# Queries computed ahead of keys and values, with their exponentials kept in memory

## The chip, the cores and the metric

The kernel runs on one core of a Trainium2 chip. A core has five engines with instruction queues of their own: TensorE (matrix products, PE in the profile, with PEld for its weight loads), VectorE (DVE), ScalarE (ACT), GpSimd (POOL) and SyncE (SP), which here only starts DMAs. The metric is the device time of one execution in microseconds; the time given is the median of several.

## The reference

For 2048 tokens of width 1024, normed to `xn`, the kernel computes a linear attention with 32 heads of width 32 and a gated feed-forward block of width 3584, and joins them:

```
q, k, v = xn @ wqkv                        # 32 heads of width 32
pq, pk  = q @ w_phi, k @ w_phi             # a 32x32 matrix for each head
phi(p)  = [softmax(p), softmax(-p)]        # 64 features for each head
kv, z   = phi(pk)^T v, sum over tokens of phi(pk)
o       = phi(pq) kv / (phi(pq) . z + 1e-6)
s       = o @ wo
g       = silu((silu(xn @ w1) * (xn @ w3)) @ w2)
out     = x + s * g
```

Everything is float32. Products run in three passes over a high and a low part of each operand (`PASSES`, `split` on lines 88 to 93): high times high, high times low, low times high, so one 128x128 block times 512 columns is three matmuls.

## The kernel before

The work goes through stages, all written out by a Python program, so every instruction has a line but no loop is left on the chip.

**Seven products.** Large products use a scheme with seven block products instead of eight (`ORDER`, line 61). The left operand of a pair of token tiles and the right operand of a pair of column halves are turned into seven sums each, named A11 ... S4 and B11 ... T4; the seven products accumulate in three PSUM banks a, b, c, and between them ScalarE copies and VectorE additions read the banks.

**Gate and up** (`gate_up`, from line 588). For each half of the tokens (`tb`) and each of 28 column blocks (`f`), seven products of twelve matmuls. Beside them runs side work, hung on event numbers by a planner: `room` (line 436) puts work only where VectorE's planned load of one product stays below 2.55 us, `at` (line 387) hangs a function on an event. The side work norms and turns the second half of x, folds `w_phi` into the key and query weights (`side_fold`), and prepares the seven sums of the key and value weights (`side_kv`), of `w2` (`side_w2`) and the high and low parts of `wo` (`side_split`), all stored in memory. Normed x is also stored plainly (`store_x`, `xn_d`).

**Keys and values** (`heads`, line 800). Two passes (`c` = 0, 1) over eight pairs of tiles. Each pair has seven products of twelve matmuls; then key features (`keys`: maximum, minimum, exponentials, sums) and the small products `kv` (line 790) with 32-column groups of TensorE. `reload` fetches x for the next pair, `fetch` the seven weight operands, 2 MB each, of the next pass.

**Down projection** (`product`, line 1031). Seven blocks `kb` over eight pairs, six matmuls a product. In the last block, tiles are gated as they come ready (`gate`: silu, stored to `g_d`) and weights of the last stage are loaded into ring slots (`ring`, line 873). Two query projections for the first tile stand among these products.

**Last stage** (lines 1179 to 1203). For each of 16 tiles: project the queries (`project_q`, 24 matmuls for each half of the columns, in the plain way with eight block products), make their features and denominators (`queries`), turn these with TensorE's transposes (`turn_e`), multiply them by the small key-value matrices (`attend`, 64x32 pieces) and finish: project with `wo` (24 matmuls a half), multiply by the gate, add x, store (`finish`).

**Order.** Where nothing is said, a scheduler orders each engine's instructions by program order and its own cost estimates. `in_order(...)` (line 47) makes the named engines follow the program text. Line 1141 does so for SyncE and TensorE; line 1202, after the first tile, leaves TensorE alone in that mode:

```
        if i == 1:
            in_order(ENG.PE)
```

An instruction waits in its engine's queue until its operands are ready, and what stands behind it waits too. That holds for SyncE's DMA starts.

Of the kernel before, what the change touches and what calls it, by code (L numbers as in the profile page):

```python
# [17 lines left out]
P = 128  # L18
# [3 lines left out]
G = 8  # L22
# [7 lines left out]
def tile_kernel(ctx: ExitStack, tc: tile.TileContext, x, wkT, wqT, wv, wphi, wo, w1, w3, w2, out):  # L30
# [39 lines left out]
    xn_d = dram.tile([P, ND, S], F, name="xn_d")  # L70
# [5 lines left out]
    wkv_d = [{n: dram.tile([P, 2, 4, 512], F, name=f"wkv_d{c}{n}") for n in BNAMES} for c in range(2)]  # L76
# [4 lines left out]
    wqo_d = [[dram.tile([P, 2, 512], F, name=f"wqo_d{c}_{k}") for k in range(ND)] for c in range(2)]  # L81
# [3 lines left out]
    z_d = dram.tile([1, 2, 4, 4, 2, DH], F, name="z_d")  # L85

# [8 lines left out]
    def project(ps, xT, w, tag="mm"):  # L95

        p = ps.tile([P, 512], F, name="pm", tag=tag, bufs=3 if tag == "mm" else BANKS["a"])
# [52 lines left out]
    HOMES = [(4, 5, 6, 0, 1, 3, 2), (7, 8, 4, 5, 6, 0, 1), (2, 3, 7, 8, 4, 5, 6), (0, 1, 2, 3, 4, 5, 6)]  # L150
# [74 lines left out]

    def store_x(t, hf, xf):
        nc.sync.dma_start(xn_d[:, 4 * hf:4 * hf + 4, t * P:(t + 1) * P], xf)
# [113 lines left out]
    def first_turn(t, h):  # L341
        q, n = t % 4, ("A11", "A12", "A21", "A22")[t // 4 * 2 + h]
        raw[q][n] = raw_x(turn(xs[t][h]), room_a[:, q] if n == "A21" else None)
        store_x(t, h, raw[q][n])
# [111 lines left out]
    def side_x(i, s0):  # L456
# [18 lines left out]
        for m, (n, j, hf) in enumerate((("A11", 0, 0), ("A12", 0, 1), ("A21", 1, 0), ("A22", 1, 1))):  # L475
            at(s1 + m, lambda n=n, j=j, hf=hf: pts.update({n: turn(xt[j][hf])}), before)
            at(s1 + m, lambda n=n: a.update({n: raw_x(pts[n])}))
            at(s1 + m + 2, lambda n=n, j=j, hf=hf: store_x(pairs[i][j], hf, a[n]))
# [10 lines left out]
    def side_kv(c, k, s0):  # L489
# [8 lines left out]
        for n in BNAMES:  # L498
# [3 lines left out]
            at_ = store_quad(at_ + 1, wkv_d[c][n][:, :, k], lambda src=src: (r + t2)[src], "wkvo", then)  # L502

    def side_fold(m, s0):
# [4 lines left out]
        if m < 16:  # L509
            at(s0 + 5, lambda: nc.scalar.copy(flat(w[0]), w[1]))  # L510
            at(s0 + 7, lambda: nc.sync.dma_start(d, flat(w[0])))
        else:
            store_quad(s0 + 5, wqo_d[c][k], lambda: w[1], "wqo")

    def side_split(d, src, s0):
        r = []

        def load():
            r.append(blk2())
# [5 lines left out]
    def side_w2(kb, kk, s0):  # L525
        r = []

        def load():
            r.extend(blk2() for _ in range(4))
            for h in range(2):  # L530
                f = 4 * kb + 2 * kk + h
                for n in range(2):
                    nc.sync.dma_start(r[h + 2 * n], w2[f * P:(f + 1) * P, n * 512:(n + 1) * 512])
# [4 lines left out]

        at(s0, load)
        at_ = room(s0 + 4, 2 * OP_US)  # L540
        at(at_, sums)
        for n in BNAMES:
# [3 lines left out]
            at_ = store_quad(at_ + 1, w2_d[kb][n][:, kk], lambda src=src: r[src], "w2o", then)  # L546
# [12 lines left out]
    for m in range(8):  # L559
        side_kv(m // 4, m % 4, FIRST_STEP + 59 + 11 * m)  # L560
    for m in range(28):
        side_store(m, FIRST_STEP + 45 + 4 * m)

    for u in range(2 * NKB):
# [678 lines left out]
```

## Time and profile before

| what | value |
|---|---|
| median of 3 runs | 2425.21 us (2424.5 to 2426.57) |
| span of the profiled execution | 2423.0 us, mean granted TensorE clock 0.999 |
| TensorE busy | 2394.2 us (99%) |
| VectorE busy | 1770.7 us (73%) |
| ScalarE busy | 881.3 us (36%) |
| GpSimd busy | 192.5 us (8%) |
| DMA | 517.87 MB, mean 214 GB/s |

The profiled execution's own time is its span, first to last instruction; the median stands 2.2 us above it. In a row of a timeline the columns are the start in us, the length in us, engine, line, operation, out<-in and the count of merged instructions; in brackets stand the idle time before and what ended it. In a row of the groups by line the columns are line, engine, operation, shapes and count, then busy us and the mean ns of one, then idle time before and what ended it. In a row by stretch of time: the stretch, its length, busy us (and count) of PE, PEld, DVE, ACT, POOL, then granted clock, share of the DMA engines and GB/s. A row of DMA issues has out<-in, queue, count, KB each and us to landing. Matmuls are pipelined: the distance between two starts, not the length of one, is what one costs.

### The profile page before, as it was taken

What the parts mean: (1) busy time and instruction counts of PE and PEld (TensorE: products, weight loads), DVE (VectorE), ACT (ScalarE), POOL (GpSimd) and SP (SyncE); (2) the same over time, 40 slices, a digit from 0 to 9 for tenths busy, and PEclk for the clock granted to TensorE, in tenths of its full rate; (3) what the DMA queues carried; (4) which work ended last, traced back from release to release, by engine and by line L of the source; (5) the groups of instructions that cost most, each with busy time, mean ns of one, the idle gap of its engine ahead of it and who ended that gap; (6) DMA issues with size and microseconds to landing.
All of it is one profiled execution on the core that took longest, in us unless ns stands there. A gap on an engine that the chain in (4) does not pass through costs nothing. (4 is left out here: it accounts for less than half of the span.)

```text
span 2423.0 us, 35675 instructions
## 1 busy us (share of the span) xinstructions
PE 2394.2 (99%) x13650; PEld 1970.2 (81%) x13650; DVE 1770.7 (73%) x2887; ACT 881.3 (36%) x1550; POOL 192.5 (8%) x158
## 2 busy tenths in 40 slices
PE   7999999999999999999999999999999999999998
PEld 6788888888888888888787888888888887888886
DVE  8877787875688878764555666678888777777775
ACT  6445444443454444442111114322222243222221
POOL 1000000000000000000000000011111112222332
PEclk9999999999999999999999999999999999999999
DMA  7456899996788876656858745442445476222221
GB/s 281 158 184 224 267 345 336 323 320 218 242 308 297 309 271 238 240 220 246 332 177 345 248 155 202 174 169 89 152 174 182 153 260 226 79 86 89 75 84 70
DMA packets 293227, 517.87 MB, mean 214 GB/s; under 512 B 18752, under 2 KB 167104, under 8 KB 291264
## 3 DMA queue, kind: packets, MB, share of 16 engines
q1 hardware_dynamic: 293056, 515.59, 61.2%
q8 instruction: 108, 1.77, 0.3%
q14 instruction: 63, 0.52, 0.1%
HBM read 329.65 MB, written 185.87 MB: 213 GB/s over the span
## 5 line engine op out<-in xcount | busy, mean ns | idle before, releaser
L93 DVE TENSOR_TENSOR bo<-rw,bo 128x512 fp32r<-128x512 f32 x336 | 230.7, 689 | 158.3 <-ACT bo L92 157.5
L92 ACT CAST bo<-rw 128x512 fp32r<-128x512 f32 x336 | 206.3, 617 | 6.2 <-DMA xo_d1S<-xoS 3.6
L1042 PE MATMUL bankb<-bo,as 128*128 128x512 f32 x816 | 200.9, 389 | 0.0
L101 PE MATMUL pm<-wq,xh 128*128 128x512 f32 x768 | 181.1, 392 | 0.0
L1042 PEld LDWEIGHTS bankb<-bo,as 128*128 128x128 f32 x816 | 153.2, 188 | 31.8
L101 PEld LDWEIGHTS pm<-wq,xh 128*128 128x128 f32 x768 | 143.1, 188 | 32.0 <-issue 2.8
L615 PE MATMUL bankb<-op0S,bo 128*128 128x512 f32 x672 | 163.0, 391 | 1.9 <-ACT op0S L92 1.1
L615 PE MATMUL bankc<-op0S,bo 128*128 128x512 f32 x672 | 162.6, 391 | 0.3 <-DVE op0S L93 0.3
L615 PE MATMUL bankb<-op1S,bo 128*128 128x512 f32 x672 | 161.2, 389 | 0.0
L615 PE MATMUL bankc<-op1S,bo 128*128 128x512 f32 x672 | 161.2, 389 | 0.0
L615 PE MATMUL bankb<-op0A,bo 128*128 128x512 f32 x672 | 159.7, 392 | 0.9 <-DVE bo L93 0.5
L615 PE MATMUL bankb<-op1A,bo 128*128 128x512 f32 x672 | 157.5, 389 | 0.1
L615 PEld LDWEIGHTS bankb<-op0S,bo 128*128 128x128 f32 x672 | 125.2, 188 | 28.5 <-ACT op0S L92 1.6
L615 PEld LDWEIGHTS bankb<-op1A,bo 128*128 128x128 f32 x672 | 126.0, 188 | 27.0 <-DVE u L657 0.9
L615 PEld LDWEIGHTS bankb<-op1S,bo 128*128 128x128 f32 x672 | 126.1, 188 | 26.2
L615 PEld LDWEIGHTS bankc<-op1S,bo 128*128 128x128 f32 x672 | 126.1, 188 | 26.2
L615 PEld LDWEIGHTS bankb<-op0A,bo 128*128 128x128 f32 x672 | 125.1, 188 | 27.0 <-DVE bo L93 0.8
L615 PEld LDWEIGHTS bankc<-op0S,bo 128*128 128x128 f32 x672 | 125.3, 188 | 26.4 <-DVE op0S L93 0.7
L101 PE MATMUL pm<-wos,oT 128*128 128x512 f32 x576 | 142.2, 397 | 4.2 <-DVE oT L93 2.7
L1042 PE MATMUL bankc<-bo,as 128*128 128x512 f32 x576 | 146.2, 389 | 0.0
L101 PEld LDWEIGHTS pm<-wos,oT 128*128 128x128 f32 x576 | 107.9, 190 | 33.3 <-DVE oT L93 9.3
L1042 PEld LDWEIGHTS bankc<-bo,as 128*128 128x128 f32 x576 | 108.1, 188 | 22.4
(233 smaller groups left out, 4245.2 us busy)
## 6 DMA issues: line engine op xcount, KB each, us to landing
rw<-in_w SPq DMA_DIRECT2D x112, 512.0 KB, 4.5
hr<-h_d SPq DMA_DIRECT2D x56, 512.0 KB, 3.6
h_d<-h SPq DMA_DIRECT2D x111, 256.0 KB, 4.6
xoS<-xo_d0S SPq DMA_DIRECT2D x32, 512.0 KB, 8.2
xoS<-xo_d1S SPq DMA_DIRECT2D x32, 512.0 KB, 3.6
room<-in_w SPq DMA_DIRECT2D x56, 256.0 KB, 6.0
xoA<-xo_d0A SPq DMA_DIRECT2D x24, 512.0 KB, 7.7
xoA<-xo_d1A SPq DMA_DIRECT2D x24, 512.0 KB, 3.5
```

What stands on the lines that cost most here:

```text
L92: nc.scalar.copy(hi, src)
L93: (by or nc.vector).tensor_sub(lo, src, hi.bitcast(F))
L101: nc.tensor.matmul(p, xT[dch][:, a], w(dch, b), start=n == 0, stop=n == 3 * ND - 1)
L615: nc.tensor.matmul(bank[b], bos[tb, f][bn][:, w, k], ao[an][:, u, k], start=first and n == 0, stop=LAST[b] == an and n == 11, skip_group_c ...
L1042: nc.tensor.matmul(bank[b], t[:, u, pos + k], bos[kb, bn, k][:, w], start=first and n == 0, stop=LAST[b] == an and n == 5, skip_group_chec ...
```

## The change

Queries get a stage of their own, ahead of keys and values, by seven products. `side_fold` stores the folded query weights plainly; four units of `side_w` (which takes the place of `side_w2`) turn them into seven sums in the second half of gate and up, among the fourteen units for `w2`. The splits of `wo` move to the first half. Normed x is no longer stored plainly. The stage loop runs over `c` = 0 (queries), 1, 2 (keys and values), with `HOMES` and `NEXT` saying which slot and which moment each operand gets.

For each pair of tiles `query_heads` makes four feature blocks; `query_features` takes maximum and minimum, subtracts (on GpSimd for three blocks of four), takes exponentials, sums them, keeps the ratio `rho` of the two sums, and stores exponentials (`e_d`, 1 MB a tile) and `rho`.

The last stage projects no queries. `load_e` loads a tile's exponentials, `prep` multiplies them by z on GpSimd, sums on VectorE, scales, and turns them in 32x32 blocks with VectorE's transpose. The first two tiles are prepared in the last block of the down projection. `attend` works on a batch of two or four tiles and one half of the columns, with 32x32 pieces, in four PSUM banks (`bufs=1`). SyncE and TensorE follow the program text through the whole stage.

```diff
+    def query_features(i, j, c, p, rho, eng):
+        e = e_rooms[j][:, c].rearrange("p (h s f) -> p h s f", s=2, f=DH)
...
+        nc.vector.tensor_reduce(mm[:, 0, :], p3, axis=AX.X, op=OP.max)
+        nc.vector.tensor_reduce(mm[:, 1, :], p3, axis=AX.X, op=OP.min)
+        eng.tensor_sub(e[:, :, 0], p3, mm[:, 0, :].unsqueeze(2).to_broadcast([P, 16, DH]))
+        eng.tensor_sub(e[:, :, 1], mm[:, 1, :].unsqueeze(2).to_broadcast([P, 16, DH]), p3)
+        nc.scalar.activation(ef, ef, AF.Exp)
+        nc.vector.tensor_reduce(sums.rearrange("p h s -> p (h s)"), ef.rearrange("p (n f) -> p n f", f=DH),
+                                axis=AX.X, op=OP.add)
+        nc.vector.reciprocal(rho[:, j, c], sums[:, :, 1])
+        nc.vector.tensor_mul(rho[:, j, c], sums[:, :, 0], rho[:, j, c])
+        nc.sync.dma_start(e_d[pairs[i][j]][:, c], ef)
...
-    late_splits = [(wqo_d[c][k], d) for _, k, c, d in folds[16:FOLDS]]
...
+    for k in range(4):
+        units.insert(4 * k + 3, ([wq_d[n][k + 4 * h] for n in range(2) for h in range(2)],
+                                 lambda n, k=k: wkv_d[0][n][:, :, k]))
+    for u, (srcs, dst) in enumerate(units):
+        side_w(srcs, dst, HALF + 4 + 8 * u)
...
-    for c in range(2):
+    NEXT = ({0: 2, 1: 3, 2: 4, 3: 5, 4: 6}, {0: 2, 1: 3, 2: 4, 3: 5, 6: 6}, {})
+    for c in range(3):
...
-            pend = heads(i, xo, wb, steps(), pend)
+            if c:
+                pend = heads(i, xo, wb, steps(), pend)
+            else:
+                query_heads(i, xo, wb, steps())
...
+    def load_e(t):
+        rhos[t] = own[0][:, 512 + 32 * (t % 4):544 + 32 * (t % 4)].rearrange("p (c h) -> p c h", c=2)
+        i, j = next((i, p.index(t)) for i, p in enumerate(pairs) if t in p)
+        nc.sync.dma_start(rhos[t], rho_d[i][:, j])
+        for c in range(2):
+            nc.sync.dma_start(e_slab(t, c), e_d[t][:, c])
+
+    def prep(t):
...
+        for c in range(2):
+            nc.gpsimd.tensor_mul(ez[c], e_slab(t, c), zb[c])
+        for c in range(2):
+            nc.vector.tensor_reduce(z[:, c].rearrange("p h s -> p (h s)"), ez[c].rearrange("p (n f) -> p n f", f=DH),
+                                    axis=AX.X, op=OP.add)
+        nc.vector.tensor_mul(den, z[:, :, :, 1], rho)
+        nc.vector.tensor_add(den, den, z[:, :, :, 0])
+        nc.vector.reciprocal(by[:, :, :, 0], den)
+        nc.vector.tensor_mul(by[:, :, :, 1], by[:, :, :, 0], rho)
+        for c in range(2):
+            e3 = e_slab(t, c).rearrange("p (n f) -> p n f", f=DH)
+            nc.vector.tensor_mul(e3, e3, by[:, c].rearrange("p h s -> p (h s)").unsqueeze(2).to_broadcast([P, H, DH]))
+            nc.vector.transpose(et_slab(t, c), e_slab(t, c))
...
+    def attend(tiles, c):
+        n = len(tiles)
+        po = ps.tile([P, 4, 512], F, name="po", bufs=1)
...
+        for k in range(4):
+            for s in range(2):
+                for j in range(4):
+                    for a in range(4):
+                        sl = slice(32 * a, 32 * a + 32)
+                        nc.tensor.matmul(ev[32 * j:32 * j + 32, a, k], kvr[c][sl, j, s, k], et[sl, :, 4 * k + j, s],
+                                         start=s == 0, stop=s == 1, skip_group_check=True)
...
+    def finish(i, c):
+        cs = slice(c * 512, c * 512 + 512)
+        g, xr = (work.tile([P, 512], F, name=name, tag="w") for name in ("g", "xr"))
+        nc.sync.dma_start(g, g_d[i][:, cs])
+        nc.sync.dma_start(xr, x[i * P:(i + 1) * P, cs])
+        p = project(ps, [oTs[i, h][:, :, k] for h in range(2) for k in range(4)], lambda k, a: wos[c, k][:, a])
+        nc.vector.tensor_mul(g, p, g)
+        (nc.vector if i + 1 == NT else nc.gpsimd).tensor_add(g, g, xr)
+        nc.sync.dma_start(out[i * P:(i + 1) * P, cs], g)
...
-        if i == 1:
-            in_order(ENG.PE)
...
+    def prepare(upto):
+        nonlocal ahead
+        while ahead < upto:
+            prep(ahead)
+            if ahead + 2 < NT:
+                load_e(ahead + 2)
+            ahead += 1
+
+    batches = [[0, 1], [2, 3], [4, 5], [6, 7], [8, 9, 10, 11], [12, 13, 14, 15]]
+    for c in range(2):
+        attend(batches[0], c)
+    done = 2
+    for tiles, later in zip(batches, batches[1:] + [None]):
+        for t in tiles:
+            for c in range(2):
+                if later and t == tiles[-1]:
+                    prepare(later[-1] + 1)
+                    attend(later, c)
+                    if c:
+                        done = later[-1] + 1
+                elif c == 0:
+                    prepare(min(ahead + 1, done + 6, NT))
+                finish(t, c)
```

More of the change, by code (lines that the diff above doesn't have):

```diff
@@ L1137, in tile_kernel @@
     ps = pool("ps4", 3, space=PSUM)
-    gate(*pairs[-1])
-    for k in range(14, 16):
-        load_wo(k, accp.tile([P, 2, 512], R, name="wos", tag="accW", bufs=2))
+    gate(len(pairs) - 1)
     in_order(ENG.SP, ENG.PE)
-    def turn_e(e, q):
-        pt = ps.tile([P, 4, P], F, name="pt2", tag="tr", bufs=3)
-        for g in range(4):
-            nc.tensor.transpose(pt[:, g, :], e[:, (4 * q + g) * P:(4 * q + g + 1) * P], ident)
-        et = work.tile([P, 4, P], F, name="et", tag="w")
-        nc.scalar.copy(et, pt)
-        return et
```

306 lines of the change are left out of this document (139 added, 167 removed).

## The prediction

> **What bounds the kernel now.** The page first: TensorE against the span.
>
> ```profile
> span 2423.0 us, 35675 instructions
> PE 2394.2 (99%) x13650; PEld 1970.2 (81%) x13650; DVE 1770.7 (73%) x2887; ACT 881.3 (36%) x1550; POOL 192.5 (8%) x158
> ```
>
> TensorE is the bound: taking matmuls away pays, as long as what replaces them keeps pace. So I read TensorE's timeline for stage borders and pitch, and the chain of waits for the end.
>
> ```profile
> 1133.71 2.88 PE L810 MATMUL bankb<-op2B,xoA 128*128 128x512 f32 x12
> 1303.69 3.01 PE L810 MATMUL bankb<-op3B,xoA 128*128 128x512 f32 x12
> 1391.46 2.88 PE L810 MATMUL banka<-op3B,xoA 128*128 128x512 f32 x12
> 1394.18 2.88 PE L810 MATMUL bankb<-op3T,xoS 128*128 128x512 f32 x12
> 1472.17 1.65 PE L1042 MATMUL bankb<-bo,af 128*128 128x512 f32 x6
> 1991.53 5.60 PE L101 MATMUL pm<-wq,xh 128*128 128x512 f32 x24
> 1996.97 1.52 PE L1042 MATMUL bankc<-bo,as 128*128 128x512 f32 x6
> 2018.12 5.60 PE L101 MATMUL pm<-wq,xh 128*128 128x512 f32 x24
> ```
>
> ```profile
> 2406.90 11.47 PE pm L101 x48
> 2418.45 0.70 DVE gx L1175
> ```
>
> Twelve matmuls take 2.72 us (1394.18 - 1391.46), a projection of 24 takes 5.44 (1996.97 - 1991.53). Gate and up end at 1133.7, keys and values at 1472.2, and the last stage runs from 2018.1 to 2418.4: 400.3 us, the stage this change rewrites.
>
> Next SyncE, with VectorE and GpSimd beside it, for the first tile of that stage, where SyncE's order is written by hand.
>
> ```profile
> 2046.32 0.34 SPq L1177 DMA_DIRECT2D out<-gx  x1
> 2046.70 0.43 SPq L1172 DMA_DIRECT2D gx<-g_d  x1
> 2047.18 0.46 SPq L1173 DMA_DIRECT2D gx<-in_x  x1
> 2052.34 0.34 SPq L1177 DMA_DIRECT2D out<-gx  x1
> ```
>
> ```profile
> 2050.22 0.69 DVE L1175 TENSOR_TENSOR gx<-pm,gx 128x512 f32<-128x512 f32 x1 [2.13 <-DMA gx<-g_d]
> ```
>
> ```profile
> 2051.04 1.27 POOL L1176 TENSOR_TENSOR gx<-gx 128x512 f32<-128x512 f32 x1 [4.75 <-DVE gx L1175]
> ```
>
> The loads of one half tile go out only after the store of the half before (2046.32, 2046.70): load, multiply, add, store, 6.0 us from store to store. TensorE needs 5.44 for the half, and VectorE sat 2.13 us for the load. Before the change this loop closes once, since SyncE's written order ends after the first tile. The diff drops that release (`if i == 1: in_order(ENG.PE)`), so the loop closes 32 times.
>
> **The change, part by part.** Terms are in the time of the profiled execution, 2423.0; the median, 2425.2, lies 2.2 higher, which I add at the end.
>
> *Gate and up.* The stores of normed x and the split query folds go; 16 splits of `wo` move to the first half, and four more units of seven quads and four sums enter the second.
>
> ```profile
> 340.00:360.00 20.00, 20.00 (x98) 16.86 (x97) 16.96 (x27) 10.32 (x19) 0.00 (x0) 1.00 1.07 383
> 860.00:980.00 120.00, 120.00 (x530) 99.06 (x529) 97.61 (x153) 57.11 (x107) 0.00 (x0) 1.00 0.77 264
> 1303.00:1313.00 10.00, 10.00 (x106) 8.37 (x106) 8.40 (x12) 2.39 (x4) 0.13 (x1) 1.00 1.01 429
> 1863.00:1939.00 76.00, 76.00 (x337) 62.95 (x336) 61.11 (x105) 20.38 (x41) 10.19 (x9) 1.00 0.42 150
> ```
>
> ```profile
> L93 DVE TENSOR_TENSOR w2o<-room,w2o 128x512 fp32r<-128x512 f32 x98 | 67.0, 684 | 0.0
> L1011 POOL TENSOR_TENSOR ez<-e,zb 128x1024 f32<-128x1024 f32 x32 | 77.3, 2416 | 211.9 <-issue 137.9 <-ACT e L1010 74.0
> L1019 DVE TENSOR_REDUCE sums<-ez 128x32 f32<-128x1024 f32 x32 | 39.0, 1220 | 39.5 <-POOL ez L1011 39.5
> L1025 DVE TENSOR_TENSOR e<-e,by 128x1024 f32<-128x1024 f32 x32 | 39.1, 1222 | 0.6
> L1023 DVE RECIPROCAL by<-rho 128x16 f32<-128x16 f32 x32 | 8.1, 253 | 1.1
> L1021 DVE TENSOR_TENSOR rho<-sums,rho 128x16 f32<-128x16 f32 x32 | 5.6, 174 | 1.0
> L795 PE MATMUL pkv<-ev 128*32 128x34 f32 x2048 | 24.6, 199 | 1.8 <-DVE ev L835 1.8
> L1159 PE MATMUL po<-et,kvu 64*32 64x128 f32 x1024 | 21.0, 277 | 0.3 <-ACT et L1150 0.3
> ```
>
> The units add 44 VectorE instructions of 0.68 us, 30, against 11 of the splits that leave. VectorE idles 22 us in each 120 there (97.6 busy), over some 460 us: cover enough, 0 us. If it were gone, 19 us would show. In the first half 16 subtractions come and 16 go, and DMA is already full in places (share 1.07); a late weight block could cost up to 5. Bounds 0 to 5; I take 0, since TensorE is busy throughout even in that row.
>
> *Queries by seven products.* A new stage of 8 pairs x 7 products x 2.72 = 152.3. Its cover: VectorE per pair has three adds, eight 512-wide reductions and two subtractions at 0.68, four 1024-wide reductions at 1.22 and eight small ones near 0.2, 15.5 us of TensorE's 19.0; if that slips, up to 8 x 2 = 16. Of GpSimd's six subtractions a pair (1.27, as at 2051.04) nothing waits but an exponential. The stored exponentials lie in the rooms of the key features; their last stores end some 5 us into the key stage, whose first use of them by TensorE comes after seven products: 0. Keys and values keep their work but no longer enter from gate and up: the first half took 170.0 against the second's 168.5, so -1.5; the entry stall is passed to queries, +1.
>
> At the hand-over to keys the operands of the next stage come in: seven of 2.1 MB, with 3.7 MB of x, while the exponentials (16 stores of 1 MB in all, 2.1 MB a pair) leave. In the row at 1303 the same hand-over already fills DMA (share 1.01, 429 GB/s) and just fits. The two last pairs now add 4.2 MB: 4.2 / 0.42 = 10 us; the earlier fetches of the diff give back some. I take 9; bounds 0 to 13.
>
> *Down projection.* Two query projections leave: -10.9. Two tiles are prepared there: per tile VectorE does two reductions, two products and two turns (6 x 1.22) and four small ones (0.8), 8.1 us. VectorE idles 14.9 us in 76 (row at 1863), 6.7 in the 34 us that are left: 16.2 - 6.7 = 9.5 at worst, 0 at best, since SyncE's loop below waits anyway. I take 3.
>
> A 32x32 turn has no row; its nearest are the 1024-wide operations, 1.22 (L1025) and 2.42 (L1011). I take 1.22, same engine and size, and 2.42 for the range: 1.2 per turn, some 5 us where a preparation is waited for. The Trainium skill, "VectorE: DVE Perf Modes", section "The three transpose paths", gives 311 ns for 128x128 bf16: an estimate of 2.5 us per turn, the sum 5 us higher.
>
> *Last stage.* TensorE: 16 x 48 matmuls, 16 x 10.9 = 174. Small products: 256 instructions in each of 12 groups (each of 128 products is two instructions, as L1159's 1024 are for 512), at 12.0 ns (24.6 / 2048) to 20.5 (21.0 / 1024): 37 to 63 us. I take 37: short columns like L795's. So TensorE needs 211 instead of 400. Turns on TensorE and their copies, splits of queries: gone with them.
>
> ```profile
> xoA<-xo_d1A SPq DMA_DIRECT2D x24, 512.0 KB, 3.5
> ```
>
> But SyncE's loop is longer. Per tile two closings, 12.0. For ten of the tiles a load of exponentials stands ahead: three DMAs to issue (about 1.35, from 0.34 to 0.46 each), 1 MB ahead of g in the queue (1.0 / 0.43 = 2.4 us, less the issue: 1.1), and one add queued behind GpSimd's 2.42 us products (0 to 4.8; I take 1.8): 16.3. Then the ends. Before tile 0's g is loaded, the load for tile 4 waits until tile 2 is prepared: 4.8 + 1.2 + 0.8 + 4.9 = 11.7, plus issue, 13. At tile 7 three tiles are prepared in one go; tile 11's load is queued behind tile 6's last store, its landing (3.5 for 512 KB by the row above, 4.5 for two) and preparation (11.7) hold TensorE and the next load: 16. Last: 10 x 16.3 + 6 x 12.0 + 13 + 16 = 264, less the 2 of add and store behind the last matmul: 262. Bounds: 217, if the loop is hidden (211 plus some 6 to empty the single PSUM room between the first groups), and 290 (below). The rest of the tail stays.
>
> Sum: 2423.0 + 152.3 + 1 - 1.5 + 9 - 10.9 + 3 - 400.3 + 262 = 2437.6; with 2.2, 2440. It breaks even at a last stage of 247.
>
> **Rivals.**
>
> *The loop is hidden (faster).* If loads go out early enough, TensorE sets the stage: 217, so 2392.6, with 2.2 2395. For it: 189 us of TensorE time leave the last stage, and only 152 come back in the query stage. Against: the row at 2050.22, a wait for exactly this load. It decides from 7.7 us per half tile down (247 / 32). The Trainium skill, "TensorE: Matmul & The Clock Gate", section "Wait — 56ns, not 53.3ns?", says starts never come closer than about 25 ns; the groups would be 77 us, this rival 2435 and no gain. The trace disagrees: 12.0 ns.
>
> *GpSimd locks VectorE out (slower still).*
>
> ```profile
> 1984.61 0.42 DVE L910 TENSOR_TENSOR s<-hr,sm 128x256 f32<-128x256 f32 x1
> 1985.88 1.52 DVE L910 TENSOR_TENSOR s<-hr,sm 128x256 f32<-128x256 f32 x1
> ...
> 2045.18 1.15 DVE L1022 TENSOR_TENSOR rho<-rho,sums 128x16 f32<-128x16 f32 x1
> ```
>
> ```profile
> 1985.65 1.46 POOL L1052 TENSOR_TENSOR acc<-acc,u 128x512 f32<-128x512 f32 x1 [7.50 <-ACT u L1051]
> ```
>
> The same subtraction takes 0.42 alone and 1.52 while GpSimd runs: it ended with GpSimd's instruction. The Trainium skill, "GPSIMD Engine Reference", section "Specifications", names this sharing for VectorE instructions with two SBUF inputs; the trace agrees. A preparation has two such products and three small ones beside 4.8 us of GpSimd: a lock of up to 2.4 for ten tiles adds 24, plus 4 at tile 7: 290, so 2465.6, with 2.2 2468. Against: in the old last stage it cost only 1.0 in a tile (L1022, 1.15 against 0.17 of its like, L1021).
>
> *The small products don't run side by side.* Then each takes the 277 ns of L1159's row by itself, 71 us a group, 850 in all: above 3200. Against: 20.5 ns a piece in that very row.
>
> **How the numbers follow.** Forecast 0.56, hidden loop 0.27, lock 0.15, no packing 0.02. The forecast's own range is 2418 to 2460 (GpSimd's queue at 0 or 3.6 a tile, hand-over 0 to 13). 0.2% of 2425 is 4.9, about what a measurement here can tell. Of the forecast one in twenty falls below -0.2% and one in eight within 0.2%; of the hidden loop 0.07 within: faster 0.28, same 0.09, slower 0.63. Range: 2393 to 2470, which leaves out about half of the hidden loop and the top of the lock.
>
> **What would show it.** Right: in SyncE's timeline of the last stage each load of g follows the store before; halves 6 us apart, tiles with exponentials 16; a gap of TensorE ahead of the small products of tile 8, over 10 us; DMA share near 1 between queries and keys. Wrong: g loads in groups ahead of the stores, or the last stage under 247 us; 32x32 instructions above 25 ns; a gap in the query stage itself.

## The result, and the profile after

The changed kernel takes 2560.61 us, median of four runs (2558.65 to 2565.31), beside 2425.89 us for the kernel before on the same chip: 1.056 times as long, 95% interval 1.0545 to 1.0575. The forecast was 2440, range 2393 to 2470: the sign was right, the time lies 120.6 us above the forecast and 90.6 above the range.

The page of the changed kernel: span, engines, the fetches of instructions (q8), and the two groups of TensorE that make the last stage.

```profile
span 2556.7 us, 39191 instructions
PE 2397.5 (94%) x15346; PEld 1965.3 (77%) x15346; DVE 1793.3 (70%) x2827; ACT 856.9 (34%) x1501; POOL 239.8 (9%) x206
...
q8 instruction: 121, 1.98, 0.3%
...
L101 PE MATMUL pm<-wos,oT 128*128 128x512 f32 x576 | 154.2, 428 | 2.9 <-DVE g L1222 2.9
...
L1208 PE MATMUL po<-acc,kvr 32*32 32x64 f32 (+1 forms) x3072 | 46.6, 283 | 80.4 <-issue 35.0
```

TensorE is busy for 94% of the span instead of 99%, and the small products (L1208) had 80.4 us of idle TensorE in front of them. TensorE's timeline gives the borders of the stages.

```profile
1143.88 2.88 PE L882 MATMUL bankb<-op2B,xoA 128*128 128x512 f32 x12
1309.72 2.66 PE L817 MATMUL bankb<-op3B,xoA 128*128 128x512 f32 x11
1667.81 1.64 PE L1106 MATMUL bankb<-bo,af 128*128 128x512 f32 x6
2223.99 2.45 PE L1208 MATMUL po<-acc,kvr 32*32 32x64 f32 x231 [0.79 <-DVE acc L1118]
```

The last matmul ends at 2547.6. Against the forecast's own terms:

| stage | before | forecast | after | missed by |
|---|---|---|---|---|
| gate and up | 1133.7 | 1133.7 | 1143.9 | 10.2 |
| queries, with entry | - | 153.3 | 165.8 | 12.5 |
| keys and values, with hand-over | 338.5 | 346.0 | 358.1 | 12.1 |
| down projection | 545.9 | 538.0 | 556.2 | 18.2 |
| last stage, to the last matmul's end | 400.3 | 262.0 | 323.6 | 61.6 |
| behind it | 4.6 | 4.6 | 9.1 | 4.5 |
| span | 2423.0 | 2437.6 | 2556.7 | 119.1 |

Every stage is longer than forecast; half of it lies in the last. By stretch of time (end of the down projection, then the last stage in three parts):

```profile
2190.00:2224.00 34.00, 24.77 (x103) 18.24 (x102) 34.00 (x48) 11.15 (x16) 9.70 (x5) 1.00 0.68 254
2224.00:2371.00 147.00, 114.51 (x2382) 93.06 (x2383) 79.18 (x102) 10.43 (x17) 43.33 (x24) 0.85 0.40 139
2371.00:2403.00 32.00, 0.68 (x3) 0.21 (x2) 20.27 (x23) 0.00 (x0) 16.38 (x8) 0.55 0.35 121
2403.00:2548.00 145.00, 125.99 (x1456) 101.03 (x1456) 53.47 (x73) 9.39 (x16) 35.06 (x22) 0.89 0.34 114
```

The granted clock, 1.00 in the old last stage, is 0.85, 0.55 and 0.89. VectorE is full (34.00 of 34.00) at the end of the down projection. The waits of TensorE in the last stage (us in total, times, longest):

```profile
PE po L1208 <- issue: 35.0, 15, 4.3
PE po L1208 <- DVE acc L1093: 31.4, 1, 31.4
PE po L1208 <- DVE oT L93: 13.2, 4, 6.2
```

**Bursts.** The 15 waits for "issue" stand inside the groups of small products: nothing that the trace shows released them. One group of 256 instructions on TensorE's timeline, and two stretches of finishing matmuls:

```profile
2256.56 1.99 PE L1208 MATMUL po<-acc,kvr 32*32 32x64 f32 x181
2260.58 0.98 PE L1208 MATMUL po<-acc,kvr 32*32 32x64 f32 x75 [2.03 <-issue]
...
2352.95 4.21 PE L101 MATMUL pm<-wos,oT 128*128 128x512 f32 x9
2356.96 3.16 PE L101 MATMUL pm<-late,oT 128*128 128x512 f32 x12
2359.95 8.32 PE L101 MATMUL pm<-wos,oT 128*128 128x512 f32 x36
```

181 products take 2 us, then nothing for 2, then the rest. Counted over all TensorE instructions of the trace (matmuls and weight loads, 30,979), 14 of the 15 pauses fall at the 193rd or 194th place of a block of 256. The q8 row above has 121 fetches of 1.98 MB, 16 KB each: one for each 256 instructions (30,979 / 121). That these are TensorE's shows in two other kernels: 27,595 instructions and 108 fetches in the kernel before, 33,017 and 129 in the run two_rooms. In the trace the fetch beside this pause starts at 2257.95 and takes 1.15 us; the pause ends 1.5 us after it. The Trainium skill, "Runtime: NRT & Kernel Launch", section "Instruction fetch mechanics", says that instructions come in blocks of 16 KiB, 256 of them, each fetched while the one before is executed, and that the cost is mostly hidden. The trace agrees on the block; in these bursts the cost is not hidden.

After pauses and waits the clock is low: 9 matmuls from 2352.95 take 4.01 us (0.446 each, to the next row's start), while 36 from 2359.95 take 8.16 (0.227). The Trainium skill, "TensorE: Matmul & The Clock Gate", section "Part 1: The HAM clock gate (the "warmup" mystery)", has the clock fall to half after an idle window of some 3.4 us; the trace's clock records agree on the two values, 1.0 and 0.5, and on steps of 3.4 us, but shorter pauses were enough here: after the one of 2.03 us above, the clock is 0.5 from 2261.9 on. It is 0.5 for 105.8 of the 323.6 us.

So the last stage is 80.9 us in the groups of small products, 194.3 in finishing matmuls (174 at full clock) and 48.5 between the two, while TensorE waits for VectorE. That is TensorE's own account; which chain of work ended last is another question.

**The loop.** SyncE in the last stage, ahead of the longest of these waits:

```profile
2365.56 0.34 SPq L1224 DMA_DIRECT2D out<-g  x1
2365.95 0.43 SPq L1071 DMA_DIRECT2D own<-rho_d  x1
2366.48 0.87 SPq L1073 DMA_DIRECT2D acc<-e_d  x2
2367.40 0.42 SPq L1219 DMA_DIRECT2D g<-g_d  x1
...
2377.21 0.34 SPq L1224 DMA_DIRECT2D out<-g  x1
```

As forecast, each load of g, and of exponentials, goes out behind a store (2365.56). In the last nine halves TensorE keeps its own pace, 49.3 us or 5.5 each, because its results have three PSUM rooms to run ahead in. The loop is slower there: six stores in 37.65 us, 6.3 each, close to the forecast's 6.0.

```profile
2506.28 0.34 SPq L1224 DMA_DIRECT2D out<-g  x1
...
2543.93 0.34 SPq L1224 DMA_DIRECT2D out<-g  x1
```

VectorE's product with g waited 53 us for loads and 7.6 for TensorE:

```profile
L1222 DVE TENSOR_TENSOR g<-pm,g 128x512 f32<-128x512 f32 x32 | 22.0, 686 | 60.5 <-DMA xr<-in_x 44.9 <-DMA g<-g_d 8.0 <-PE pm L101 7.6
```

In the chain of waits that ended last, followed back from the end to 2224, DMA has 28%, GpSimd 17% and TensorE's matmuls 15%. The loop also runs through work that the forecast put beside it. At tile 3 the chain goes from a load of exponentials (2303.30) over GpSimd's product, a preparation and the split of a group of small products (2321.40) to the product with g (2323.24) and the store (2325.37). From the last store of one tile to the last of the next, tiles 2, 4, 6, 8 and 9 take 17.0 to 18.1 us. The tiles in which a group of small products stands take longer: 25.9, 23.0 and 22.8 for tiles 1, 3 and 5, 58.1 for tile 7, with the wait of 31.4 ahead of tile 8 in it. At the very end the loop still runs on behind the last matmul:

```profile
2549.32 0.43 SPq L1219
...
2549.80 3.04 DMA xr<-in_x
```

**Hand-over from queries to keys.** ScalarE, then VectorE:

```profile
1341.56 0.59 ACT L830 COPY ev<-bankb 128x512 f32<-128x512 f32 x1 [25.18 <-DMA rho_d<-rho]
```

```profile
1341.43 0.69 DVE L112 TENSOR_TENSOR ev<-k,mm 128x512 f32<-128x512 f32 x1 [22.42 <-DMA e_d<-eq]
```

Both stood for over 22 us, until the last pair's exponentials were stored, because keys write into the same two rooms; TensorE stood 14.2 us, as ScalarE could not empty a bank.

### The profile page after: what moved, and what is told of

Read it like the earlier page. It is cut to its first block, busy times and chain, and to the rows that moved or that the text cites. A ratio compares the mean times of both kernels' runs of the same rounds, so it can differ in the third digit from the quotient of the medians.

```text
span 2556.7 us, 39191 instructions
## 1 busy us (share of the span) xinstructions
PE 2397.5 (94%) x15346; PEld 1965.3 (77%) x15346; DVE 1793.3 (70%) x2827; ACT 856.9 (34%) x1501; POOL 239.8 (9%) x206
## 3 DMA queue, kind: packets, MB, share of 16 engines
q8 instruction: 121, 1.98, 0.3%
## 4 chain that ended last, share of the span: by engine, by line
PE 77%; DMA 9%; DVE 7%; issue 3%; POOL 2%; ACT 1%; SPq 1%; POOLq 0%; DVEq 0%; ACTq 0%
PE bankb L622 22%; PE bankb L1106 11%; PE bankc L622 11%; PE bankb L817 7%; PE banka L622 6%; PE bankc L1106 5%; PE bankc L817 3%; PE banka L1106 3%; PE bankb L882 2%; DMA acc<-e_d 2%; PE banka L817 2%; DMA xr<-in_x 1%; POOL ez L1082 1%; PE pm L101 1%; POOL g L1223 1%
## 5 line engine op out<-in xcount | busy, mean ns | idle before, releaser
L93 DVE TENSOR_TENSOR bo<-rw,bo 128x512 fp32r<-128x512 f32 x336 | 230.9, 689 | 160.2 <-ACT bo L92 158.5
L101 PE MATMUL pm<-wos,oT 128*128 128x512 f32 x576 | 154.2, 428 | 2.9 <-DVE g L1222 2.9
L101 PEld LDWEIGHTS pm<-wos,oT 128*128 128x128 f32 x576 | 119.0, 209 | 31.6 <-DVE g L1222 3.3
L862 POOL TENSOR_TENSOR eq<-q,mm 128x512 f32<-128x512 f32 x24 | 25.3, 1053 | 1220.9 <-DVE mm L860 1163.4
L1208 PE MATMUL po<-acc,kvr 32*32 32x64 f32 (+1 forms) x3072 | 46.6, 283 | 80.4 <-issue 35.0
```

Of the source, the lines that this page charges most:

```text
L93: (by or nc.vector).tensor_sub(lo, src, hi.bitcast(F))
L101: nc.tensor.matmul(p, xT[dch][:, a], w(dch, b), start=n == 0, stop=n == 3 * ND - 1)
L862: eng.tensor_sub(e[:, :, 0], p3, mm[:, 0, :].unsqueeze(2).to_broadcast([P, 16, DH]))
L1208: nc.tensor.matmul(ev[32 * j:32 * j + 32, a, k], kvr[c][sl, j, s, k], et[sl, :, 4 * k + j, s], start=s == 0, stop=s == 1, skip_group_check ...
```

## The experiments

Against the changed kernel, in medians of four runs each; the stages in us are from the profiled execution. The kernel before lay between 2423.3 and 2425.8 beside them.

| run | time | to before (95%) | gate, up | queries | keys | down | last |
|---|---|---|---|---|---|---|---|
| the change | 2560.6 | 1.0545 to 1.0575 | 1143.9 | 165.8 | 189.9 | 556.2 | 323.6 |
| sync_free | 2525.8 | 1.0410 to 1.0441 | 1145.2 | 167.9 | 187.7 | 555.7 | 294.0 |
| early_prep | 2545.8 | 1.0486 to 1.0520 | 1143.6 | 166.0 | 190.1 | 555.9 | 304.4 |
| spread | 2569.7 | 1.0594 to 1.0629 | 1144.1 | 165.4 | 190.2 | 556.0 | 331.4 |
| ev_room | 2552.3 | 1.0515 to 1.0547 | 1146.0 | 165.9 | 180.6 | 555.6 | 323.5 |
| wo_late | 2555.3 | 1.0521 to 1.0552 | 1135.6 | 166.3 | 190.8 | 551.8 | 328.8 |
| preps_late | 2556.3 | 1.0528 to 1.0559 | 1143.0 | 165.7 | 190.3 | 549.1 | 326.7 |
| no_store | 2533.1 | 1.0426 to 1.0461 | 1147.6 | 158.9 | 166.9 | 556.1 | 324.9 |
| two_rooms | 2525.0 | 1.0395 to 1.0426 | 1145.5 | 166.4 | 190.2 | 557.7 | 289.7 |
| all_mended | 2498.9 | 1.0299 to 1.0333 | 1135.6 | 166.6 | 179.9 | 550.8 | 288.7 |
| hr_first | 2567.1 | 1.0569 to 1.0604 | 1145.2 | 166.7 | 190.4 | 557.7 | 322.5 |
| no_z | 2479.3 | 1.0206 to 1.0236 | 1137.2 | 166.5 | 179.3 | 547.0 | 274.0 |
| preps_out | 2564.8 | 1.0562 to 1.0598 | 1144.9 | 166.4 | 188.0 | 548.2 | 337.3 |
| no_prep | 2494.0 | 1.0269 to 1.0303 | 1144.4 | 166.6 | 190.2 | 540.9 | 271.1 |
| no_z_alone | 2530.2 | 1.0417 to 1.0448 | 1144.6 | 166.8 | 188.5 | 549.8 | 302.3 |

("keys" is the first half of keys and values.) A stage that an edit leaves alone moves by up to some 5 us from kernel to kernel (in wo_late the down projection is 4.4 shorter and the last stage 5.2 longer).

**SyncE released (sync_free).**

```diff
-    in_order(ENG.SP, ENG.PE)
+    in_order(ENG.PE)
```

> Only SyncE is taken out of the hand-written order in the last stage, so that loads of g, x and of the exponentials can pass the stores of results. By the recorded working (the loop load g, multiply, add, store sets 6.0 us a half tile and 16 us a tile with exponentials) the last stage, 323.6 us from the first small product to the last matmul, falls by some 45 us to 100 us. By the reading of the new trace (TensorE sets the halves: the last nine take 5.5 us each; the loop holds up only the exponentials of tiles 8 to 11) it falls by 25 to 45 us, nearly all of it the 31.5 us gap ahead of the small products of tile 8, and the clock that drops behind that gap. If neither, that gap stays and the time moves by less than 5 us.

34.8 us less: the last stage falls by 29.6 and the tail behind it from 9.1 to 4.6. The price of the loop is thus 34, in the range of the second reading; the 45 to 100 of the first are too much. With the loop gone the stage still takes 294.0: 77.1 in small products, 188.7 in finishing matmuls, 28.2 waiting. Of the 31.4 us ahead of tile 8 nothing is left, but TensorE now waits 28.2 us in three places for the emptying of the small products' PSUM (L93), which VectorE has behind its preparations.

**Preparations earlier (early_prep).**

```diff
+    UPTO = (3, 4, 6, 7, 9, 10, 11, 12, 13, 14, 15, 16, 16, 16, 16, 16)
-                    prepare(later[-1] + 1)
+                    prepare(UPTO[t])
...
-                    prepare(min(ahead + 1, done + 6, NT))
+                    prepare(UPTO[t])
```

> The preparations of tiles 4 to 11 are issued earlier and evenly (at most two ahead of a tile) instead of three in a row at tile 7; SyncE keeps its order. If the 31.5 us gap comes from three preparations being issued together, it shrinks by 15 to 30 us. If it comes from SyncE's loop, in which each load of exponentials stands behind the store of a result, the gap only moves to an earlier tile and the time changes by less than 8 us.

14.8 less, at the lower edge of the first reading, and not all of the gap (19.2 in the last stage, but the profiled execution was 5.9 us faster than the median). The wait ahead of the first group of tile 8 is gone; between the two halves of the columns, waits of 6.0, 6.5 and 15.4 us come up at tiles 4, 6 and 8. Part of the gap was the three preparations in a row, part the late loads.

**Bursts broken up (spread).**

```diff
             for s in range(2):
...
+            if k < 3:
+                yield
...
+                if n % 4 == 0:
+                    next(small, None)
                 nc.tensor.matmul(p, xT[dch][:, a], w(dch, b), start=n == 0, stop=n == 3 * ND - 1)
...
-                    attend(later, c)
+                    finish(t, c, attend(later, c))
```

> Each group of 128 small products is issued in four parts of 32, with four finishing matmuls between two parts, instead of in one burst. If the pauses inside the groups (15 of them, 0.9 to 4.5 us, all but one at the same place of a block of 256 TensorE instructions) are waits for instructions, they go, except in the first two groups, which stay bursts: 20 to 35 us less, and a clock nearer to 1. If a 32x32 product takes its 23 ns by itself (weights, PSUM), groups and stage stay within 8 us of what they were.

The pauses go, as the fetch reading has it; the time does not, it grows by 9.1. A group on TensorE's timeline:

```profile
2256.34 0.85 PE L1210 MATMUL po<-acc,kvr 32*32 32x64 f32 x64
2257.13 1.19 PE L103 MATMUL pm<-wos,oT 128*128 128x512 f32 x4
...
2262.04 0.85 PE L1210 MATMUL po<-acc,kvr 32*32 32x64 f32 x64
2262.83 3.00 PE L103 MATMUL pm<-wos,oT 128*128 128x512 f32 x12
2274.28 1.09 PE L1210 MATMUL po<-acc,kvr 32*32 32x64 f32 x64 [8.46 <-DVE oT L93]
```

and its waits:

```profile
PE po L1210 <- DVE oT L93: 47.1, 5, 10.0
...
PE po L1210 <- issue: 12.1, 4, 4.2
```

64 instructions take 0.79 us (12.3 ns each, the forecast's price), and the four pauses left are those of the first two groups, still bursts. All groups together take 57.4 us instead of 80.9. But a group now ends 12 matmuls before the next one wants the same PSUM, instead of 24, and the waits for its emptying grow from 13.2 to 47.1 us. So groups that are 23.5 us shorter did not make this stage shorter.

**A room for the first keys (ev_room).**

```diff
+        if not key_rooms:
+            two = big.tile([P, 2, 2048], F, name="evs", tag="big5")
+            key_rooms.extend([two[:, 0], two[:, 1], None])
+        t = key_rooms.pop(0) if len(key_rooms) > 1 else rwp.tile([P, 2048], F, name="ev", tag="rw")
```

> The exponentials and values of the first pair of keys go to a slot of weights that is free by then, instead of to the two rooms that the queries' exponentials leave only when their stores have landed. If the room is what holds TensorE up at the hand-over, the gap of 14.3 us goes and the first half of keys and values falls from 189.9 by 13 to 20 us. If the full DMA queues are, TensorE waits a few us later for operands instead, and less than 5 us is won.

8.3 less, 9.3 in the first half of keys and values, between the two readings. The gap of 14.2 is gone; waits for weight operands from memory (6.8 us instead of 5.3) and small ones remain. The room was about half of the excess (9.3 of 19.6).

**Splits of `wo` late again (wo_late).**

```diff
-    for m in range(2 * ND):
-        c, k = divmod(m, ND)
-        side_split(wo_d[c][k], ..., FIRST_STEP + 64 + 11 * m // 2)
...
+        if u < 2 * ND:
+            c, k = divmod(u, ND)
+            side_split(wo_d[c][k], ..., HALF + 8 + 8 * u)
```

> The splits of the output weights go back into the second half of gate and up. If their move is what added 10.2 us to gate and up (waits of 1.0 to 1.6 us on ScalarE and VectorE between 350 and 480 us), the stage falls by 6 to 10 us and the whole time with it. If the queries' weights, now folded there, or the removed stores of x did it, the stage stays within 3 us or the waits only move to the second half.

Gate and up falls by 8.3 to 1135.6. The stretch where TensorE had waited, in the change and then in this run:

```profile
350.00:400.00 50.00, 45.50 (x209) 36.92 (x208) 39.37 (x62) 26.21 (x49) 0.00 (x0) 1.00 1.05 384
```

```profile
350.00:400.00 50.00, 50.00 (x234) 41.85 (x233) 42.50 (x67) 25.34 (x48) 0.00 (x0) 1.00 1.02 346
```

The move of the splits was the cause; which of its loads, stores or subtractions, these rows do not tell (the edit also puts their input into the rooms of the other side work). The whole falls by 5.3 only: the last stage came out 5.2 longer in this run and the down projection 4.4 shorter, neither of which the edit touches.

**Preparations out of the down projection (preps_late, preps_out, hr_first).** First, the two calls moved:

```diff
-                prep(0)
-                load_e(2)
...
+    for t in range(2):
+        prep(t)
+        load_e(t + 2)
```

> The preparations of tiles 0 and 1 leave the down projection and stand at the start of the last stage. If they are what lengthens the down projection beyond its 535 us without queries (VectorE is busy 34.0 of its last 34.0 us), it falls by 15 to 21 us, and the first small products wait some 20 to 25 us instead: the whole is 0 to 12 us slower. If the loads and the reading of weights at the end of the down projection do it, the stage falls by less than 6 us and the whole is 15 to 25 us slower.

The scheduler put the first sums where they had been (2150.9 instead of 2151.2), so little was moved; the down projection falls by 7.1, little more than it moves by itself, and the whole by 4.3. Then also the loads:

```diff
-                load_e(0)
...
+    load_e(0)
+    load_e(1)
     for t in range(2):
```

> In the run with late preparations the planner still ran them in the down projection. Here the loads of exponentials of tiles 0 and 1 are issued only at the start of the last stage, so that no preparation can run before. If the preparations (and the loads and GpSimd work they bring) are the down projection's excess, it falls from 556.2 to 535 to 541 us, and the last stage grows by 20 to 32 us (a load of 5 us, two preparations of 10.8 us of VectorE each). If kernel order, gates or weights are, the down projection stays above 548 us and the whole is 15 to 30 us slower.

Down 8.0 less, last stage 13.7 more; again the scheduler issued these loads and GpSimd's products in the down projection. VectorE there, then GpSimd:

```profile
2149.91 2.50 DVE L93 TENSOR_TENSOR as<-sm,as 128x256 fp32r<-128x256 f32 x1
...
2153.74 2.56 DVE L972 TENSOR_TENSOR s<-hr,sm 128x256 f32<-128x256 f32 x1
```

```profile
2149.73 2.40 POOL L1082 TENSOR_TENSOR ez<-acc,zb 128x1024 f32<-128x1024 f32 x1 [5.42 <-DVE af L93]
...
2153.50 2.52 POOL L1082 TENSOR_TENSOR ez<-acc,zb 128x1024 f32<-128x1024 f32 x1
```

Each subtraction, 0.42 us by itself, lasts as long as GpSimd's product beside it; TensorE then waits 4.9 us. Another suspicion was the queue of SyncE:

```diff
-            nc.sync.dma_start(g_d[t], slabs[:, m])
+            later.append(lambda m=m, t=t: nc.sync.dma_start(g_d[t], slabs[:, m]))
...
             first = a_first(*steps[r + 1])
+        while later:
+            later.pop(0)()
```

> In the down projection the stores of the gates and the loads of exponentials of a step are issued after the next step's load of h, instead of before it on SyncE's hand-ordered queue. If the waits of TensorE in the last 75 us of the down projection (2.6 and 2.7 us at 2149 and 2153, and those up to 2222) come from h loads that stand behind these issues, the down projection falls from 556.2 by 6 to 14 us. If they come from VectorE, which the two preparations fill, it falls by less than 4 us.

The down projection does not fall (557.7) and the whole is 6.5 slower: TensorE waits as long in that stage (15.2 us after 15.1), 11.7 of it for `as`, a split on VectorE. That theory falls.

**Without preparations, and without GpSimd's product (no_prep, no_z_alone).**

```diff
     def prep(t):
-        rho = rhos.pop(t)
-        at_ = 256 * (t % 2)
...
+        rhos.pop(t)
```

> Left out of the changed kernel: all preparations (product with z, sums, factors, turns); the exponentials are still loaded, the small products read what lies in the slabs, and the output is not the reference's. If the preparations are the down projection's excess, it falls from 556.2 to 535 to 541 us. In the last stage the 31.5 us gap goes, but the bursts stay: by the reading of the trace 24 groups' worth of small products keep 70 to 80 us, the last stage is 270 to 290 us. If the bursts were slowed by VectorE's or GpSimd's work beside them, they shrink to some 40 us and the stage to 215 to 240 us.

The down projection falls by 15.3 to 540.9, inside the range: the preparations are 15.3 of the 21.2 us that it has beyond 535.0, and 5.9 stay open. The last stage falls to 271.1, also inside, 264.6 of it TensorE's own (78.1 and 186.5); the groups of small products still take 78.1 us with neither VectorE nor GpSimd preparing anything:

```profile
PE po L1191 <- issue: 35.1, 14, 4.5
...
PE po L1191 <- DVE oT L93: 6.5, 2, 5.2
```

So the bursts are slow by themselves.

```diff
-            nc.gpsimd.tensor_mul(ez[c], e_slab(t, c), zb[c])
...
-            nc.vector.tensor_reduce(..., ez[c].rearrange("p (n f) -> p n f", f=DH),
+            nc.vector.tensor_reduce(..., e_slab(t, c).rearrange("p (n f) -> p n f", f=DH),
```

> Left out of the changed kernel: GpSimd's product of exponentials and z alone; the output is not the reference's. If it is mainly GpSimd that locks VectorE, the down projection falls by 8 to 14 us and the last stage by 10 to 25 us. If VectorE's own work in the preparations counts, the down projection falls by less than 5 us, and the last stage by less than 10.

30.4 less: 6.4 in the down projection (between the two readings), 21.3 in the last stage (inside the first). GpSimd's product is some 40% of what the preparations cost in either stage (6.4 of 15.3, 21.3 of 52.5). In the last stage little of this is VectorE being locked out. The two small operations that the lock stretches there take, in the changed kernel, 0.25 (L1086) and 0.60 us instead of 0.19, some 6 us over 13 tiles:

```profile
L1087 DVE TENSOR_TENSOR own<-own 128x32 f32<-128x32 f32 x13 | 7.8, 601 | 0.4
```

The rest fits the product's own 2.4 us, twice a tile, in the chain that ends last; no run separates the two.

**The stores of exponentials (no_store).**

```diff
-        nc.sync.dma_start(e_d[pairs[i][j]][:, c], ef)
+        if i == 0:
+            nc.sync.dma_start(e_d[pairs[0][j]][:, c], ef)
...
-            nc.sync.dma_start(e_slab(t, c), e_d[t][:, c])
+            nc.sync.dma_start(e_slab(t, c), e_d[pairs[0][j]][:, c])
```

> Left out: the stores of the exponentials of all query pairs but the first, whose exponentials every tile then loads; the output is not the reference's. If the 14.7 MB written are what the query stage and the hand-over pay for, the query stage falls from 165.8 to 153 to 157 us and the first half of keys and values from 189.9 to 168 to 173, together some 27 to 35 us. If the reading of operands alone fills the queues, less than 10 us goes.

27.5 less: 23.0 in keys and values, whose whole excess it is, and 6.9 in the query stage, together as the first reading has it. Of TensorE's two waits there, in the changed kernel,

```profile
PE bankb L882 <- DMA xoA<-xo_d1A: 4.9, 1, 4.9
PE bankb L882 <- DMA xoA<-xo_d0A: 3.6, 1, 3.6
```

the first goes and the one at the entry (3.8 in this run) stays. With the stores the DMA engines are busy for 0.90 of the query stage:

```profile
1143.90:1309.70 165.80, 157.26 (x673) 128.71 (x672) 111.87 (x189) 46.45 (x56) 48.59 (x47) 0.97 0.90 340
```

**Mended together (two_rooms, all_mended, no_z).** SyncE released, bursts broken up, batches of two throughout, and each half of the columns in its own part of the PSUM:

```diff
-        po = ps.tile([P, 4, 512], F, name="po", bufs=1)
-        ev = po[:, :, :4 * n * DH].rearrange(...)
+        ev = po[:, :, 256 * c:256 * c + 4 * n * DH].rearrange(...)
...
+        prepare(min(t + 3, NT))
+        for c in range(2):
+            if t % 2 and t + 1 < NT:
+                finish(t, c, attend([t + 1, t + 2], c))
```

> Last stage alone: SyncE free, batches of two tiles all through, each group of small products in four parts among finishing matmuls, and the two column halves with PSUM regions of their own, so that a group never waits for the emptying of the one before. The three terms of the excess, bursts (some 43 us), loop (some 35 us) and emptying of PSUM (some 14 us), should then add up: the last stage falls from 323.6 to 215 to 245 us, the whole to 2450 to 2485 us. If VectorE takes over as the bound (13.5 us of its work in each of 14 tiles, beside 12.6 us on TensorE) it stays above 250 us.

The terms do not add up: 289.7, hardly below SyncE's release alone (294.0). TensorE waits 31.2 us for VectorE (L93). With VectorE's order written by hand, a preparation in two parts three tiles ahead, and the edits of ev_room and wo_late:

```diff
-    in_order(ENG.SP, ENG.PE)
+    in_order(ENG.PE, ENG.DVE)
...
+            next(turns, None)
```

> As the run with two rooms, and VectorE too in a hand-written order in the last stage: the emptying of the small products' PSUM and the product with g stand ahead of the preparations, which are cut in two parts, one behind each half tile, three tiles ahead; with it the first keys' own room and the late splits of the output weights. If what held the two-room version up was the order on VectorE (emptying queued behind a whole preparation), the last stage falls from 289.7 to 235 to 255 us (some 19 us of bursts, 13 tiles at 13.5 to 14.5 us of VectorE, 3 at 12.6 us of TensorE), and with 8 us each from the other two edits the whole is 2445 to 2475 us. If it is the amount of work on VectorE, stretched while GpSimd runs, the last stage stays above 270 us and the whole above 2490 us.

2498.9 us, the fastest of the kernels that leave nothing out, and still 1.032 times the kernel before. The last stage does not move (288.7): the order was not the matter. VectorE's small operations in that stage (10 tiles), where L1096 and L1097 are one product and one addition of a preparation and L1099 a product of the same size:

```profile
L1096 DVE TENSOR_TENSOR own<-own 128x32 f32<-128x32 f32 x10 | 14.8, 1477 | 0.3
L1097 DVE TENSOR_TENSOR own<-own 128x32 f32<-128x32 f32 x10 | 12.4, 1243 | 0.3
...
L1099 DVE TENSOR_TENSOR own<-own 128x32 f32<-128x32 f32 x10 | 1.9, 194 | 0.3
```

2.3 us a tile go to standing beside GpSimd. Next, GpSimd's product left out. The kernel that ran is not quite the one that the expectation names: VectorE's order is not written by hand in it and the preparations are not cut in two, so it is two_rooms with the edits of ev_room and wo_late, without the product. The same two lines in it:

> The all-mended kernel without GpSimd's product of exponentials and z (4.8 us a tile); the sums are taken over the exponentials themselves, so the output is not the reference's. VectorE's own work stays the same, 13.5 us a tile. If VectorE instructions stretched while GpSimd runs (the small products take 1.48 and 1.24 us there against 0.19) set the pace, the last stage falls from 288.7 by 25 to 45 us. If VectorE's own work or the order of waiting sets it, it falls by less than 10 us.

```profile
L1097 DVE TENSOR_TENSOR own<-own 128x32 f32<-128x32 f32 x8 | 2.5, 317 | 0.1
L1096 DVE TENSOR_TENSOR own<-own 128x32 f32<-128x32 f32 x8 | 1.4, 174 | 0.0
```

Against all_mended 19.6 less, 14.7 of it in the last stage; against two_rooms, which has the same order, 15.7 in the last stage: between the two readings either way. The lock is real. What holds the other 274.0 us above the 225 that TensorE alone needs (174, and 64 pieces of 0.79) is not shown: it waits 16.7 us for VectorE's splits, the groups take 65.1 instead of 50.6 us, the finishing matmuls 192.2 instead of 174. (The 13.5 us a tile in these expectations is too high for VectorE's own work: six operations of 1.22, four small ones, two splits and two products with g, 0.68 each, make 10.9; 13.6 is what it takes in all_mended with the lock.)

## Why the prediction was wrong

**The last stage, 262: the longer of two sums, TensorE's 211 and the loop's 262, as if they ran side by side.** This step failed most. Both sums were too small, and they have steps in common.

**TensorE's 211, and with it the rival's 217.** With the loop out of the way (sync_free) the stage takes 294.0: small products 77.1 for 37, finishing matmuls 188.7 for 174, waits for VectorE 28.2 for some 6. So 262 was out of reach at any price of the loop. The term most mis-sized is "I take 37: short columns like L795's", 80.9 in the changed kernel. The price of 12.0 ns was right for what that row shows, runs of 64 instructions between products of twelve matmuls, and spread gives it back (12.3). It was carried over to runs of 256 and 512, which outrun the supply of instructions. The forecast's own mark for this, 32x32 instructions above 25 ns, came true (80.9 / 3072 = 26 ns). The 174 became 194.3: the price is one at full clock, and a TensorE that pauses ran at half clock for 105.8 us of this stage. By TensorE's own account these two terms are 64 us more than forecast. That the stage would be shorter by as much without them is not shown: spread took 23.5 off the groups, and the stage grew by 7.8.

**SyncE's loop** was seen rightly: loads behind stores, 6.3 us a half at the end (6.0 said), 17.0 to 18.1 for tiles with exponentials and no group (16.3 said). But 264 for the whole loop became 329.7, and 59 of these 66 us lie in the six tiles at which a group of small products stands (0, 1, 3, 5, 7, 11). As shown for tile 3, the product with g there comes behind a preparation, a group and its split; the forecast had counted a preparation in the loop only at the start and at tile 7. At tile 7, 31.4 us of TensorE's waiting stood where 16 was said. That 51 us of waiting was forecast (262 less 211) and 48.5 stood there is chance, as 28.2 remain without the loop. So is part of the right sign: the release is worth 34, and without the loop the change is still 1.042 times as long.

**"0" for the rooms of the exponentials at the hand-over.** "Their last stores end some 5 us into the key stage" was 32 (1341.5 less 1309.7), and TensorE meets the room not after seven products but as soon as ScalarE cannot copy a bank into it. With DMA this was given 9 in all; the excess of keys and values was 19.6 against before. Taking the stores away gives back 23.0, the room by itself 9.3.

**Queries, 152.3, with nothing for DMA.** Cover was looked for on VectorE and GpSimd, and held there. What failed was the load of operands: 8.5 us of waits, then half clock. Without the stores half of the miss goes (6.9).

**Down projection, "I take 3".** Bounds were 0 to 9.5; the preparations cost 15.3, and 5.9 more stay open. The "0 at best, since SyncE's loop below waits anyway" was wrong. The worst case had left out GpSimd's products, which stretch whatever VectorE does beside them, not only the preparation's own lines; without them the 8.9 that remain lie inside the bounds.

**Gate and up, "I take 0".** Bounds 0 to 5, measured 10.2; the clue, DMA at 1.07 in that stretch, was quoted and set aside. Undoing the move gave 8.3 back.

**The lock, a rival at 0.15,** has the size that was given (2.3 us a tile) in all_mended; in the last stage of the changed kernel it is some 0.5 a tile. GpSimd's product as a whole, its own time included, accounts for 27.7 us over both stages. "No packing" falls.

Whether a version of this change can win: all_mended has 1.9 us more than before in gate and up, 166.6 in queries, 9.7 in keys and values, 4.9 in the down projection, and 111.6 less in the last stage. To break even the last stage would have to take 217 us. In that arrangement TensorE alone needs 174 and 64 pieces of 0.79, 225. Not tried: fewer, larger small products, and sums over z made elsewhere than on VectorE and GpSimd.

## What to carry to other kernels

A price per instruction holds for the length of run in which it was measured: ask what supplies instructions when hundreds of short ones stand together, and put long ones between them (here the groups fell from 80.9 to 57.4 us, though not the stage). Taking the longer of two sums assumes that no step stands in both: follow one round of the slower loop through every engine it passes. When matmuls are taken from the busiest engine, price what remains at the clock it will get with the new pauses in it, and give every engine that becomes nearly full (here VectorE beside GpSimd, and DMA) its own line in the sum. A room that is free "when the store has landed" is as late as the DMA queue is long.

## What the runs showed of the hardware

- Bursts of 32x32 products stop at one place in blocks of 256 TensorE instructions, 15 times in 12 groups of 512 (weight loads among them), for 0.5 to 4.3 us, 14 of the 15 at the same place of a block. Runs of 64 with four 128x512 matmuls between them did not stop in spread; they did three times in two_rooms (0.7 to 1.8 us), five times in no_z and twice in all_mended (0.2 to 0.8).
- A 32x32 turn of 128x1024 float32 on VectorE takes 1.22 us, as the 1024-wide arithmetic does (group by lines, last stage of the changed kernel):

```profile
L1093 DVE STREAM_TRANSPOSE acc<-acc 128x1024 f32<-128x1024 f32 x28 | 33.5, 1224 | 0.1
```

The estimate of 2.5 us from the Trainium skill, "VectorE: DVE Perf Modes", section "The three transpose paths", is not borne out here.
- VectorE instructions that read two operands from SBUF wait for GpSimd's to end (0.42 us becomes 2.50 in preps_out, 0.19 becomes 1.48 in all_mended), the splits of the down projection too.
